# Moving a weight product ahead of the attention in a fused attention and FFN kernel

## The chip, the cores and the metric

The kernel runs on one core of one Trainium2 chip. The time is device microseconds of one execution; the time before is the median of 12 runs. A profile shows one execution: TensorE (PE, with its weight loads as PEld), VectorE (DVE), ScalarE (ACT), GpSimd (POOL), SyncE (SP) and the DMA queues.

## The reference

```python
# q, k, v: 8 batches x 8 heads x 576 positions x 64, fp32
r = max(x, 0);  phi(x) = [r * cos(theta_s), r * sin(theta_s)]      # 128 features per position
kv  = sum over s of phi(k)[s] (x) v[s]        # per batch and head, 128 x 64
den = phi(q) . sum over s of phi(k)[s] + 1e-6
attn = (phi(q) @ kv) / den                    # -> x, 4608 x 512
h = ((x @ w1) * (x @ w2)) @ w3                # w1, w2: 512 x 1024; w3: 1024 x 1024
out = h @ w_out                               # w_out: 1024 x 512; out: 4608 x 512, fp32
```

## The kernel before

The kernel folds the last two products: it computes `w34 = w3 @ w_out` (1024 x 512) once and then, per token, `((x @ w1) * (x @ w2)) @ w34`. All products are in bf16 with fp32 sums.

**Order.** The Tile framework's own scheduling is switched off: each engine runs its instructions in the order in which the program emits them. Tokens are worked in nine blocks of 512 (`t` = 0 to 8). `ffn_groups(t)` is a generator that stops after each group of FFN matmuls; block t has 24 groups, numbered from 0. Groups 0 to 15 of a block make the products with w1 and w2: for feature columns of 128, `aT` with w1 is copied by ACT to `asb`, and DVE multiplies it with `bT` into `abT`. Groups 16 to 23 multiply `abT` with `w34b`, two groups to a row tile, and ACT copies the result to `osb`. The main loop keeps a list of small steps for each group, `slots[g]`, and emits them right behind the group. So the attention of the next batch, and what prepares it, is threaded between the FFN's groups.

**Attention of a batch b.** It goes in five row tiles `c` (four of 128 rows, one of 64): `prep_k` and `prep_q` make the features (the cosine half on DVE, the sine half on ACT, by `features`), `prep_v` copies v beside a column of ones into `va`. `kv_chunk` accumulates k-v sums of eight heads in the PSUM tile `pnum`; its last call copies them to `kvs`. `q_tr` transposes a q tile on PE and copies it to `qpT`; `num` multiplies it with `kvs` and emits the den chain on DVE (add, reciprocal, multiply into `xblk`); `x_tr` transposes `xblk` into the FFN's input `xT`. `pnum` has one buffer, the transposes' tile `pst` two, the FFN's PSUM tile four.

**The start.** Batch 0's k is loaded in fp32 by SP (`kf`); v, q, and the rest are loaded by POOL with a cast to bf16. PE runs 27 idle matmuls on a tile of zeros (`idle_mms`). When k and v are there, batch 0's features and `kv_first()` follow (the k-v sums in two PSUM tiles, copied to `kvs` by ACT in two halves), then the first three q tiles with four more idle matmuls between, and block 0 of the FFN starts. `other_loads` holds back the remaining loads until the first `xblk` is made: the last quarters of w1 and w2, all of w_out in one DMA, w3 in eight row blocks of 128, batches 1 and 2.

**w34.** For each row block `jp` of w3, `w3_tr(jp)` transposes it on PE in eight pieces, DVE copies it to `w3T` (two buffers), and `w34_mm(jp, part)` multiplies it with w_out in two halves of four matmuls; behind the second half ACT copies the sum to `w34b`. Before, all of this stands in block 0 behind group 15 (the first transposes behind group 14), and the features, transposes and k-v sums of batch 1 are threaded between its sixteen halves.

Of the kernel before, what the change touches and what calls it, by code (L numbers as in the profile page):

```python
# [68 lines left out]
def kernel(  # L69
# [26 lines left out]
    ps_att = ctx.enter_context(tc.tile_pool(name="ps_att", bufs=1, space=bass.MemoryType.PSUM))  # L96
    ps_tr = ctx.enter_context(tc.tile_pool(name="ps_tr", bufs=2, space=bass.MemoryType.PSUM))
    first = [ctx.enter_context(ExitStack()) for _ in range(2)]
    ps_idle = first[1].enter_context(tc.tile_pool(name="ps_idle", bufs=1, space=bass.MemoryType.PSUM))
    ps_first = first[0].enter_context(tc.tile_pool(name="ps_first", bufs=1, space=bass.MemoryType.PSUM))  # L100

    ctx.enter_context(tc.manual_schedule())
# [7 lines left out]
    def load_first(eng, t, src, c0=0, n=4, b=0):  # L110
        rows = src[b, :, 0:512, :].rearrange("h (p j) d -> p h j d", j=4)
        eng.dma_start(out=t[:, :, c0:c0 + n, :].rearrange("p h j d -> p h (j d)"),
                      in_=rows[:, :, c0:c0 + n, :].rearrange("p h j d -> p h (j d)"))

    def load_first4(eng, t, src, b=0):
        eng.dma_start(out=t[0:64, :, 4, :], in_=src[b, :, 512:S, :].rearrange("h p d -> p h d"))
# [29 lines left out]
    def load_w3(jp):  # L146
        nc.gpsimd.dma_start(out=w3b[:, jp, :], in_=moe_w3[ts(jp, P), :])

    k0 = raw[0, "k"] = wst.tile([P, H, NCH, D], FP32, name="kf", bufs=1)
    q0 = raw[0, "q"] = ld.tile([P, H, NCH, D], BF16, name="qs")  # L150
    v0 = raw[0, "v"] = ld.tile([P, H, NCH, D], BF16, name="vs")
    load_first(nc.sync, k0, k)
    load_first4(nc.sync, k0, k)
    load_first(nc.gpsimd, v0, v)
    zeros = const.tile([P, 512], BF16, name="zeros")
    nc.vector.memset(zeros[:], 0.0)
    va_bufs, kp_bufs, qp_bufs = [], [], []
# [9 lines left out]
            nc.vector.memset(fp[64:128, 4, :, :], 0.0)  # L167
            bufs.append(fp)

    feature_buffers(0)  # L170
    tiny = const.tile([P, 1], FP32, name="tiny")
    nc.scalar.activation(out=tiny[:], in_=zeros[:, 0:1], func=ACTF.Relu, scale=1.0, bias=0.0)

    unread = ps_idle.tile([P, 512], FP32, name="unread")
    kva = ps_idle.tile([P, 512], FP32, name="kva")

    def idle_mms(n):

        for _ in range(n):
            nc.tensor.matmul(unread[:, :], lhsT=zeros[:, 0:128], rhs=zeros[:], start=True, stop=True)  # L180

    idle_mms(27)
    cosv, sinv = _trig_tables(nc, const)
    identb = const.tile([P, P], BF16, name="identb")
    load_first4(nc.gpsimd, v0, v)
    load_first(nc.gpsimd, q0, q, 0, 2)
    make_identity(nc, identb[:])
    load_first(nc.gpsimd, q0, q, 2, 2)
    def load_w12(c0, n):
        nc.gpsimd.dma_start(out=w1b[:, :, ds(c0, n)], in_=w1v[:, :, ds(c0, n)])  # L190
        nc.gpsimd.dma_start(out=w2b[:, :, ds(c0, n)], in_=w2v[:, :, ds(c0, n)])
# [6 lines left out]
    def other_loads(behind):  # L198

        seen = sm.tile([P, 1], BF16, name="seen", bufs=1)  # L200
        nc.gpsimd.tensor_copy(out=seen[:], in_=behind)
        nc.gpsimd.dma_start(out=w2b[:, :, ds(512, 256)], in_=w2v[:, :, ds(512, 256)])
        load_w12(768, 256)
        nc.gpsimd.dma_start(out=woutb[:], in_=moe_w_out.rearrange("(c p) m -> p c m", p=P))
        for jp in range(8):
            load_w3(jp)
            if jp == 4:
                load(1, "k")
        load(1, "qv")
        load(2, "kqv")  # L210


# [11 lines left out]

    def w34_mm(jp, part):
        if part == 0:
            w34_acc[jp] = ffn_tile()
        acc, w3T = w34_acc[jp], w3Ts[jp]
        for lc in range(4 * part, 4 * part + 4):
            nc.tensor.matmul(acc[:, :], lhsT=w3T[:, lc, :], rhs=woutb[:, lc, :],  # L230
                             start=(lc == 0), stop=(lc == 7))
        if part == 1:
            nc.scalar.copy(out=w34b[:, jp, :], in_=acc[:, :])
# [38 lines left out]
                                        op0=ALU.max, op1=ALU.mult)  # L272

    def prep_k(b, c):
        features(b, feat_of(b)[0], raw[b, "k"], c)

    def prep_q(b, c):
        features(b, feat_of(b)[1], raw[b, "q"], c)
# [10 lines left out]
    def kv_chunk(b, c, i):  # L289
# [8 lines left out]
        if i == NCH - 1:  # L298
# [1 line left out]
            nc.vector.tensor_copy(out=kvs[:].rearrange("p (g h) e -> p g (h e)", g=2),  # L300
                                  in_=kvt[:, :, 0:260])
            att[b]["kvs"] = kvs

    def kv_first():

        kp, qp, va = feat[0]
        kvs = sm.tile([P, H, D + 1], BF16, name="kvs", bufs=2)
        kvb = ps_att.tile([P, 2, 512], FP32, name="pnum")
        halves = (kva[:, :], kvb[:, 0, :])
        for c in range(NCH):  # L310
            for h in range(H):
                nc.tensor.matmul(halves[h // 4][:, ds((h % 4) * 65, 65)], lhsT=kp[:, c, h, :],  # L312
                                 rhs=va[:, c, h, 0:D + 1], start=(c == 0 and h % 4 == 0),
                                 stop=(c == NCH - 1 and h % 4 == 3))
        att_of(0)["kvs"] = kvs
        yield
        for half in range(2):
            nc.scalar.copy(out=kvs[:, 4 * half:4 * half + 4, :], in_=halves[half][:, 0:260])
        yield

    def q_tr(b, c, evac=True):
        R = ROWS[c]
# [117 lines left out]
    def ffn_tile():  # L440
        pool = ps_ffn[ffn_tiles[0] // 2 % 2]
        ffn_tiles[0] += 1
        return pool.tile([P, 512], FP32, name="ffnps")
# [118 lines left out]
            slots[min(last, first + int(i * (last + 1 - first) / len(units)))].append(u)  # L562


    for c in range(NCH):
        prep_k(0, c)
    for c in range(NCH):
        prep_v(0, c)
    kv_steps = kv_first()
    next(kv_steps)  # L570
    q0f = feat[0][1]
    features(0, q0f, q0, 0, scalar_heads=4)
    next(kv_steps)
    prep_q(0, 1)
    idle_mms(2)
    q_tr_halves(0, 0)
    prep_q(0, 2)
    idle_mms(1)
    num(0, 0)
    q_tr(0, 1, evac=False)[1]()  # L580
    other_loads(att[0]["x"][0][:, 0, 0, 0:1])
    features(0, q0f, q0, 3, sin=False)
    q_tr(0, 2, evac=False)[1]()
    features(0, q0f, q0, 3, cos=False)
    idle_mms(1)
    x_tr(0, 0, by_vector=True,
         pst=unread[:, :].bitcast(BF16).rearrange("p (a b) -> p a b", b=128))
    num(0, 1)
    ps_ffn = []
    for stack in first:  # L590
# [5 lines left out]
    for t in range(NT):  # L596
        slots = [[] for _ in range(24)]
        if t == 0:
            slots[1].append(lambda: x_tr(0, 1, by_vector=True))
            slots[1].append(lambda: q_tr(0, 3, evac=False)[1]())  # L600
            slots[1].append(lambda: num(0, 2))
            slots[3].append(lambda: num(0, 3))
            slots[3].append(lambda: x_tr(0, 2))
            slots[5].append(lambda: x_tr(0, 3))
            slots[6].append(lambda: prep_q(0, 4))
            slots[11].append(lambda: feature_buffers(1))
            slots[8].append(lambda: q_tr(0, 4))
            slots[10].append(lambda: num(0, 4))
            slots[12].append(lambda: x_tr(0, 4))
            slots[14].append(lambda: w3_tr(0))  # L610
            between = [[] for _ in range(32)]
            later = [[] for _ in range(24)]
            spread(prep_units(1, (prep_k,)), 6, 8, between)
            spread(prep_units(1, (prep_q,)), 10, 12, between)
            spread(prep_units(1, (prep_v,)), 13, 13, between)
            attention_at(1, between, kv=(14, 14, 14, 14, 15), tr=(12, 13, 17, 18, 19),
                         nu=(16, 17, 18, 20, 22), xt=(18, 19, 20, 22, 25))
            later[:8] = between[24:32]
            for jp in range(8):
                for part in range(2):  # L620
                    if part == 0 and jp < 7:
                        slots[15].append(lambda jp=jp: w3_tr(jp + 1))
                    slots[15].append(lambda jp=jp, part=part: w34_mm(jp, part))
                    slots[15] += between[2 * jp + part]
            for g in range(16, 24):
                slots[g] += between[g]
            slots[16].append(open_held)
            slots[16].append(lambda: load(3, "kqv"))
            spread(prep_units(2, (prep_k,)), 20, 23, slots)
        elif t == 1:  # L630
            for g in range(24):
                slots[g] += later[g]
            spread(prep_units(2, (prep_q,)), 0, 4, slots)
            spread(prep_units(2, (prep_v,)), 0, 4, slots)
            attention_at(2, slots, kv=(2, 3, 4, 5, 6), tr=(3, 5, 7, 9, 11),
                         nu=(8, 10, 12, 14, 16), xt=(8, 10, 12, 14, 16))
            slots[4].append(lambda: load_piece(4, 0, feat[2][1], 3))
            spread(interleaved(3, range(1, 6)), 6, 23, slots)
        else:
            if t + 1 < B:  # L640
                attention_at(t + 1, slots, kv=(0, 1, 2, 3, 4), tr=(2, 4, 7, 10, 13),
                             nu=(6, 8, 10, 12, 14), xt=(6, 8, 10, 12, 14))
            for g in {5: (3, 9, 15, 20), 6: (1, 6, 11, 16)}.get(t, ()):
                slots[g].append(store_held)
            if t + 2 < B:
                spread(interleaved(t + 2), 0, 22, slots)
        for g, _ in enumerate(ffn_groups(t)):
            for u in slots[g]:
                u()
# [30 lines left out]
```

## Time and profile before

| | us |
|---|---|
| median of 12 runs (lowest to highest) | 251.63 (251.08 to 253.7) |
| profiled execution, its own time | 251.62 |
| its span, first to last instruction | 249.3 |
| busy in the span: PE, DVE, ACT, POOL | 241.3, 141.4, 124.3, 90.0 |
| first FFN matmul | 15.70 |
| first matmul of token block 1 | 63.42 |
| mean granted clock of TensorE over the span | 0.997 |

The span leaves out 2.3 us of the execution's time. Busy times of PE are modelled ends of pipelined matmuls. All times in the text are counted from the start of the span.

### The profile page before, as it was taken

The numbers are of one execution on the slowest core, as the hardware profiler recorded it, in microseconds if no ns is written. First come the engines' busy times: TensorE is split into PE (matmuls) and PEld (weight loads), VectorE is DVE, ScalarE is ACT, GpSimd is POOL, SyncE is SP. The second block draws the span as 40 slices with busy tenths as digits, with TensorE's granted clock in tenths as the row PEclk, the third lists the DMA queues.
The fourth block names the chain that finished last, engine by engine and source line by source line (L and its number), as shares of the span: only waits on it lengthen the run. The fifth ranks groups of instructions, "written<-read, shape, count | busy, mean of one in ns | idle before, by whom it ended". The sixth has DMA issues, their size and how long they took to land.

```text
span 249.3 us, 4941 instructions
## 1 busy us (share of the span) xinstructions
PE 241.3 (97%) x1847; PEld 130.1 (52%) x1879; DVE 141.4 (57%) x338; ACT 124.3 (50%) x209; POOL 90.0 (36%) x171
## 2 busy tenths in 40 slices
PE   8899999999999999999999999999999999999994
PEld 3578555666555455445544554555455544444443
DVE  7875665657889529905981695189227704312321
ACT  2676316915966656465655555555432242323320
POOL 7665154540533613441443327271342540023000
PEclk9999999999999999999999999999999999999998
DMA  7999999999999999999899979999699982014013
GB/s 194 182 194 201 208 204 205 198 199 198 269 137 169 181 170 130 173 199 171 127 129 190 182 100 188 146 186 192 130 141 196 266 232 64 3 32 136 1 44 127
DMA packets 80760, 39.85 MB, mean 160 GB/s; under 512 B 48224, under 2 KB 77280, under 8 KB 80736
## 3 DMA queue, kind: packets, MB, share of 16 engines
q0 software_dynamic: 37024, 27.20, 71.2%
q1 hardware_dynamic: 43280, 11.87, 31.7%
q10 hardware_dynamic: 432, 0.46, 0.5%
q8 instruction: 15, 0.25, 0.4%
q14 instruction: 9, 0.07, 0.1%
HBM read 38.80 MB, written 9.44 MB: 193 GB/s over the span
## 4 chain that ended last, share of the span: by engine, by line
PE 93%; DMA 2%; ACT 2%; issue 1%; DVE 1%; ACTq 0%
PE ffnps L462 49%; PE ffnps L508 24%; PE ffnps L230 5%; PE pnum L353 4%; PE pnum L295 4%; DMA kf<-in_k_dram 2%; PE pst L326 2%; PE pst L218 1%; ACT kp L267 1%; PE pst L390 1%; PE ffnps L531 1%; PE kva L312 0%; DVE xblk L363 0%; PE pnum L312 0%; PE pfirst L353 0%
## 5 line engine op out<-in xcount | busy, mean ns | idle before, releaser
L503 DVE TENSOR_TENSOR abT<-asb,ffnps 128x512 bf16<-128x512 bf16 x68 | 46.4, 683 | 71.4 <-PE ffnps L462 70.6
L462 PE MATMUL ffnps<-xT,w1b 128*128 128x512 bf16 (+2 forms) x313 | 74.4, 357 | 0.7 <-ACT xT L392 0.2
L462 PE MATMUL ffnps<-xT,w2b 128*128 128x512 bf16 (+2 forms) x305 | 73.1, 356 | 0.7
L499 ACT CAST asb<-ffnps 128x512 bf16<-128x512 f32 x68 | 39.8, 585 | 61.7 <-PE ffnps L462 56.1
L508 PE MATMUL ffnps<-w34b,abT 128*128 128x512 bf16 x274 | 62.4, 379 | 0.3
L462 PEld LDWEIGHTS <-w1b 128*128 128x128 bf16 x320 | 29.4, 98 | 29.6 <-issue 0.6
L508 PEld LDWEIGHTS <-abT 128*128 128x128 bf16 x280 | 26.8, 98 | 31.2
L462 PEld LDWEIGHTS <-w2b 128*128 128x128 bf16 x320 | 26.9, 98 | 20.3
L267 ACT ACTIVATE qp<-qs,sinv 128x512 bf16<-128x512 bf16 (+2 forms) x40 | 28.3, 718 | 1.6 <-DMA qs<-in_q_dram 1.6
L363 DVE TENSOR_TENSOR xblk<-pnum,den 128x512 bf16<-128x512 f32 (+1 forms) x39 | 26.9, 691 | 1.4
L287 POOL COPY va<-vs 128x512 bf16<-128x512 bf16 (+1 forms) x30 | 18.3, 622 | 20.3 <-DMA vs<-in_v_dram 11.6
L436 POOL DMA_DIRECT2D out_dram<-osb x20 | 10.6, 533 | 41.3 <-ACT osb L518 41.3
L267 ACT ACTIVATE kp<-ks,sinv 128x512 bf16<-128x512 bf16 (+1 forms) x35 | 24.7, 721 | 0.0
L518 ACT COPY osb<-ffnps 128x512 f32<-128x512 f32 x19 | 11.1, 584 | 21.9 <-PE ffnps L508 19.9
L353 PEld LDWEIGHTS <-qpT 128*128 128x128 bf16 x320 | 15.1, 98 | 8.6 <-issue 0.9
L295 PEld LDWEIGHTS <-kp 128*128 128x128 bf16 x280 | 13.1, 98 | 7.1
L263 DVE TENSOR_SCALAR qp<-qs,cosv 128x512 bf16<-128x512 bf16 (+1 forms) x40 | 16.2, 411 | 0.6 <-DMA qs<-in_q_dram 0.6
L518 ACT COPY held<-ffnps 128x512 f32<-128x512 f32 x16 | 9.4, 585 | 14.4 <-PE ffnps L508 14.4
L353 PE MATMUL pnum<-kvs,qpT 128*128 128x65 bf16 x312 | 16.5, 194 | 0.0
L544 POOL COPY seen<-kp 128x1 bf16<-128x1 bf16 (+1 forms) x20 | 3.7, 186 | 33.3 <-DVE kp L263 25.6
L230 PE MATMUL ffnps<-woutb,w3T 128*128 128x512 bf16 x61 | 15.0, 379 | 0.1
L436 POOL DMA_DIRECT2D out_dram<-held x22 | 11.6, 535 | 8.2 <-DMA out_dram<-osb 6.5
(88 smaller groups left out, 197.3 us busy)
## 6 DMA issues: line engine op xcount, KB each, us to landing
out_dram<-held POOLq DMA_DIRECT2D x10, 256.0 KB, 5.3
qs<-in_q_dram POOLq DMA_DIRECT2D x8, 256.0 KB, 7.9
w3b<-in_moe_w_dram POOLq DMA_DIRECT2D x8, 256.0 KB, 13.5
ks<-in_k_dram POOLq DMA_DIRECT2D x6, 320.0 KB, 10.7
qs<-in_q_dram POOLq DMA_DIRECT2D x6, 320.0 KB, 9.0
vs<-in_v_dram POOLq DMA_DIRECT2D x6, 320.0 KB, 8.7
ks<-in_k_dram POOLq DMA_DIRECT2D x6, 256.0 KB, 9.0
vs<-in_v_dram POOLq DMA_DIRECT2D x6, 256.0 KB, 9.5
```

Source lines behind the costliest of these rows:

```text
L230: nc.tensor.matmul(acc[:, :], lhsT=w3T[:, lc, :], rhs=woutb[:, lc, :], start=(lc == 0), stop=(lc == 7))
L267: nc.scalar.activation(out=dst[:R, c, 0:n, D:F], in_=src[:R, 0:n, c, :], func=ACTF.Relu, scale=sinv[:R, at:at + 1], bias=0.0)
L287: eng.tensor_copy(out=feat_of(b)[2][:R, c, :, 0:D], in_=raw[b, "v"][:R, :, c, :])
L295: nc.tensor.matmul(kvt[:, h // 4, ds((h % 4) * 65, 65)], lhsT=kp[:, c, h, :], rhs=va[:, c, h, 0:D + 1], start=(i == 0 and h % 4 == 0), sto ...
L353: nc.tensor.matmul(nt[:, h // 4, ds((h % 4) * 65, 65)], lhsT=qpT[:, h, ds(at, 128)], rhs=kvs[:, h, :], start=True, stop=True)
L363: nc.vector.tensor_tensor(out=xblk[rows], in0=n4[:, :, :, 0:D], in1=den[rows].unsqueeze(3).to_broadcast([R, 2, 4, D]), op=ALU.mult)
L436: eng.dma_start(out=rows[:, :, cols], in_=osb[64 * i:64 * i + rows.shape[0], :, cols])
L462: nc.tensor.matmul(out, lhsT=w[:, kc, ts(jc, 128)], rhs=x[:, kc, tok], start=(kc == 0), stop=(kc == 3))
L499: nc.scalar.copy(out=asb[:], in_=aT[:, :])
L503: nc.vector.tensor_mul(out=abT[:, jc, :], in0=asb[:], in1=bT[:, :])
L508: nc.tensor.matmul(ops[:, :], lhsT=abT[:, jc, ts(ms, 128)], rhs=w34b[:, jc, :], start=(jc == 0), stop=(jc == 7))
L518: nc.scalar.copy(out=osb[:, ms % 2, :], in_=ops[:, :])
```

## The change

`w34` is computed first. PE runs 12 idle matmuls, then the transposes and products of w3's row blocks as they arrive; batch 0's features, k-v sums and q tiles follow behind block 6, with the second half of block 7's product between the first q transposes and the first `num`. `kv_first()` is gone, and batch 0 uses `kv_chunk` like the others, with one copy to `kvs` on DVE. Its k comes by POOL with a cast, like v and q; of the k sines ACT makes six heads and DVE two. The first four row blocks of w_out (half of it) are loaded in fp32 by SP and cast by four ACT copies, the other four by POOL with a cast. POOL's order is w3 blocks 0 and 1, half of w_out, w3 blocks 2 to 6, k, w3 block 7, v, q, then w1 and w2 as before. The two sets of feature buffers (`feature_buffers`, memsets on DVE) are made between the blocks. In block 0 the features of batch 1 stand in groups 9 to 16, its k-v sums in 13 to 15, and its q transposes in 16 to 19. The w34 sums have a PSUM pool of their own (`ps_w34`, two buffers) that is given back, with the tile of the first `num`, before the FFN's tiles are made.

```diff
+    woutf = wst.tile([P, 4, DM], FP32, name="woutf", bufs=1)
+    woutv = moe_w_out.rearrange("(c p) m -> p c m", p=P)
+    for half in range(2):
+        nc.sync.dma_start(out=woutf[:, ts(half, 2), :], in_=woutv[:, ts(half, 2), :])
+    load_w3(0)
+    k0, q0, v0 = (ld.tile([P, H, NCH, D], BF16, name=name + "s") for name in "kqv")
-    load_first(nc.sync, k0, k)
-    load_first4(nc.sync, k0, k)
-    load_first(nc.gpsimd, v0, v)
...
-    idle_mms(27)
+    idle_mms(12)
+    load_w3(1)
+    identb = const.tile([P, P], BF16, name="identb")
+    make_identity(nc, identb[:])
+    nc.gpsimd.dma_start(out=woutb[:, 4:8, :], in_=woutv[:, 4:8, :])
     cosv, sinv = _trig_tables(nc, const)
+    for lc in range(4):
+        nc.scalar.copy(out=woutb[:, lc, :], in_=woutf[:, lc, :])
+    for jp in range(2, 7):
+        load_w3(jp)
+    load_first(nc.gpsimd, k0, k)
+    load_first4(nc.gpsimd, k0, k)
+    load_w3(7)
+    load_first(nc.gpsimd, v0, v)
     load_first4(nc.gpsimd, v0, v)
     load_first(nc.gpsimd, q0, q, 0, 2)
     load_first(nc.gpsimd, q0, q, 2, 2)
...
-        nc.gpsimd.dma_start(out=woutb[:], in_=moe_w_out.rearrange("(c p) m -> p c m", p=P))
-        for jp in range(8):
-            load_w3(jp)
-            if jp == 4:
-                load(1, "k")
-        load(1, "qv")
+        load(1, "kvq")
         load(2, "kqv")
...
-        features(b, feat_of(b)[0], raw[b, "k"], c)
+        features(b, feat_of(b)[0], raw[b, "k"], c, scalar_heads=6 if b == 0 else H)
...
-    for c in range(NCH):
-        prep_k(0, c)
+    w3_tr(0)
+    w3_tr(1)
+    w34_mm(0, 0)
+    w34_mm(1, 0)
+    w34_mm(0, 1)
+    w3_tr(2)
+    w34_mm(1, 1)
+    feature_buffers(0)
+    for jp in range(2, 7):
+        w3_tr(jp + 1)
+        w34_mm(jp, 0)
+        w34_mm(jp, 1)
+        if jp == 3:
+            feature_buffers(1)
+        if jp == 5:
+            for c in range(NCH):
+                prep_k(0, c)
+    w34_mm(7, 0)
     for c in range(NCH):
         prep_v(0, c)
-    kv_steps = kv_first()
-    next(kv_steps)
-    q0f = feat[0][1]
+        kv_chunk(0, c, c)
+    q0f = feat_of(0)[1]
     features(0, q0f, q0, 0, scalar_heads=4)
-    next(kv_steps)
     prep_q(0, 1)
-    idle_mms(2)
     q_tr_halves(0, 0)
     prep_q(0, 2)
-    idle_mms(1)
+    w34_mm(7, 1)
     num(0, 0)
...
-            spread(prep_units(1, (prep_k,)), 6, 8, between)
-            spread(prep_units(1, (prep_q,)), 10, 12, between)
-            spread(prep_units(1, (prep_v,)), 13, 13, between)
...
+            spread(prep_units(1, (prep_k,)), 9, 11, slots)
+            spread(prep_units(1, (prep_v,)), 12, 13, slots)
+            spread(prep_units(1, (prep_q,)), 14, 16, slots)
+            attention_at(1, later, kv=(13, 13, 14, 14, 15), tr=(16, 17, 17, 18, 19),
+                         nu=(17, 18, 19, 20, 22), xt=(19, 20, 21, 22, 25))
```

In the lines left out, `w34_mm` takes its PSUM tile from `ps_w34`, the last idle matmul goes, and the first `x_tr` takes its tile from `ps_w34` too.

More of the change, by code (lines that the diff above doesn't have):

```diff
@@ L98 @@
     first = [ctx.enter_context(ExitStack()) for _ in range(2)]
-    ps_idle = first[1].enter_context(tc.tile_pool(name="ps_idle", bufs=1, space=bass.MemoryType.PSUM))
+    ps_w34 = first[1].enter_context(tc.tile_pool(name="ps_w34", bufs=2, space=bass.MemoryType.PSUM))
     ps_first = first[0].enter_context(tc.tile_pool(name="ps_first", bufs=1, space=bass.MemoryType.PSUM))
@@ L147, in load_w3 @@
         nc.gpsimd.dma_start(out=w3b[:, jp, :], in_=moe_w3[ts(jp, P), :])
-    k0 = raw[0, "k"] = wst.tile([P, H, NCH, D], FP32, name="kf", bufs=1)
-    q0 = raw[0, "q"] = ld.tile([P, H, NCH, D], BF16, name="qs")
-    v0 = raw[0, "v"] = ld.tile([P, H, NCH, D], BF16, name="vs")
-    load_first(nc.sync, k0, k)
-    load_first4(nc.sync, k0, k)
-    load_first(nc.gpsimd, v0, v)
+    woutf = wst.tile([P, 4, DM], FP32, name="woutf", bufs=1)
[4 more added lines that the diff above has]
+    k0, q0, v0 = (ld.tile([P, H, NCH, D], BF16, name=name + "s") for name in "kqv")
+    raw.update({(0, "k"): k0, (0, "q"): q0, (0, "v"): v0})
     zeros = const.tile([P, 512], BF16, name="zeros")
@@ L168, in feature_buffers @@
             bufs.append(fp)
-    feature_buffers(0)
     tiny = const.tile([P, 1], FP32, name="tiny")
     nc.scalar.activation(out=tiny[:], in_=zeros[:, 0:1], func=ACTF.Relu, scale=1.0, bias=0.0)
-    unread = ps_idle.tile([P, 512], FP32, name="unread")
-    kva = ps_idle.tile([P, 512], FP32, name="kva")
+    unread = ps_w34.tile([P, 512], FP32, name="acc")
     def idle_mms(n):
@@ L180, in idle_mms @@
             nc.tensor.matmul(unread[:, :], lhsT=zeros[:, 0:128], rhs=zeros[:], start=True, stop=True)
-    idle_mms(27)
-    cosv, sinv = _trig_tables(nc, const)
-    identb = const.tile([P, P], BF16, name="identb")
+    idle_mms(12)
[3 more added lines that the diff above has]
+    nc.gpsimd.dma_start(out=woutb[:, 4:8, :], in_=woutv[:, 4:8, :])
+    cosv, sinv = _trig_tables(nc, const)
+    for lc in range(4):
[6 more added lines that the diff above has]
+    load_first(nc.gpsimd, v0, v)
     load_first4(nc.gpsimd, v0, v)
     load_first(nc.gpsimd, q0, q, 0, 2)
-    make_identity(nc, identb[:])
     load_first(nc.gpsimd, q0, q, 2, 2)
@@ L226, in w34_mm @@
         if part == 0:
-            w34_acc[jp] = ffn_tile()
+            w34_acc[jp] = ps_w34.tile([P, 512], FP32, name="acc")
         acc, w3T = w34_acc[jp], w3Ts[jp]
@@ L302, in kv_chunk @@
             att[b]["kvs"] = kvs
[L304 to L309, printed above, removed]
-        for c in range(NCH):
[L311 to L319, printed above, removed]
     def q_tr(b, c, evac=True):
@@ L562, in spread @@
             slots[min(last, first + int(i * (last + 1 - first) / len(units)))].append(u)
-    for c in range(NCH):
-        prep_k(0, c)
+    w3_tr(0)
[16 more added lines that the diff above has]
+    w34_mm(7, 0)
     for c in range(NCH):
         prep_v(0, c)
-    kv_steps = kv_first()
-    next(kv_steps)
-    q0f = feat[0][1]
+        kv_chunk(0, c, c)
+    q0f = feat_of(0)[1]
     features(0, q0f, q0, 0, scalar_heads=4)
-    next(kv_steps)
     prep_q(0, 1)
-    idle_mms(2)
     q_tr_halves(0, 0)
     prep_q(0, 2)
-    idle_mms(1)
+    w34_mm(7, 1)
     num(0, 0)
@@ L584 @@
     features(0, q0f, q0, 3, cos=False)
-    idle_mms(1)
     x_tr(0, 0, by_vector=True,
-         pst=unread[:, :].bitcast(BF16).rearrange("p (a b) -> p a b", b=128))
+         pst=ps_w34.tile([P, 512], FP32, name="acc")[:, :].bitcast(BF16).rearrange("p (a b) -> p a b", b=128))
     num(0, 1)
@@ L605 @@
             slots[6].append(lambda: prep_q(0, 4))
-            slots[11].append(lambda: feature_buffers(1))
             slots[8].append(lambda: q_tr(0, 4))
@@ L609 @@
             slots[12].append(lambda: x_tr(0, 4))
-            slots[14].append(lambda: w3_tr(0))
-            between = [[] for _ in range(32)]
-            later = [[] for _ in range(24)]
-            spread(prep_units(1, (prep_k,)), 6, 8, between)
-            spread(prep_units(1, (prep_q,)), 10, 12, between)
-            spread(prep_units(1, (prep_v,)), 13, 13, between)
[L616 to L626, printed above, removed]
+            later = [[] for _ in range(32)]
+            spread(prep_units(1, (prep_k,)), 9, 11, slots)
[3 more added lines that the diff above has]
+                         nu=(17, 18, 19, 20, 22), xt=(19, 20, 21, 22, 25))
+            for g in range(24):
+                slots[g] += later[g]
+            later = later[24:]
             slots[16].append(open_held)
@@ L630 @@
         elif t == 1:
-            for g in range(24):
-                slots[g] += later[g]
+            for g, units in enumerate(later):
+                slots[g] += units
             spread(prep_units(2, (prep_q,)), 0, 4, slots)
```

## The prediction

> **What bounds it now.** I read the page first, then stretches, then the chain of waits, then single engines.
>
> ```profile
> PE 241.3 (97%) x1847; PEld 130.1 (52%) x1879; DVE 141.4 (57%) x338; ACT 124.3 (50%) x209; POOL 90.0 (36%) x171
> PE 93%; DMA 2%; ACT 2%; issue 1%; DVE 1%; ACTq 0%
> 0.00:15.70 15.70, 13.17 (x114) 6.91 (x116) 12.20 (x42) 8.59 (x14) 9.93 (x22) 1.00 1.27 190
> 15.70:63.40 47.70, 47.04 (x474) 30.99 (x481) 31.09 (x75) 24.52 (x43) 19.80 (x31) 1.00 1.34 201
> 32.00:50.00 18.00, 17.84 (x141) 10.63 (x143) 11.25 (x27) 10.71 (x18) 8.97 (x14) 1.00 1.29 202
> ```
>
> TensorE (PE) is busy 97% and is 93% of the chain, so only PE work removed, or PE waiting, moves the end. In the stretches the columns after the length are PE, its weight loads, DVE, ACT, POOL. From 15.7 us on PE is full. Before 15.7 most of its 13.17 us is the idle matmuls (L180), which do nothing. The row 32 to 50 is where w3 @ w_out is computed, with batch 1's preparation between: DVE has 7 us free there and ACT 7 us.
>
> ```profile
> 0.74 6.14 DMA kf<-in_k_dram
> 6.97 3.18 ACT kp L267 x5
> ...
> 15.70 1.05 PE ffnps L462 x16
> ...
> 33.52 0.45 PE pst L218 x8
> 33.97 1.73 PE ffnps L230 x8
> ...
> 63.42 1.73 PE ffnps L462 x8
> ```
>
> This chain (start, length, what) gives the frame. The FFN starts at 15.70, token block 1 at 63.42. One block of w3 costs PE 0.45 + 1.73 = 2.18 us, all eight 17.4 us. The change takes these out of block 0 and puts them ahead of the FFN. If nothing else moved, the FFN could start at 15.70 + 17.4 = **33.1 us** with the end unchanged. That is the break-even.
>
> **When w3 arrives.** POOL issues a further cast DMA when an older one has landed, so its waits show the pace of the queue:
>
> ```profile
> 24.56 0.69 POOL L134 DMA_DIRECT2D ks<-in_k_dram  x1 [0.64 <-DMA w2b<-in_moe_w_dram]
> 30.31 0.56 POOL L147 DMA_DIRECT2D w3b<-in_moe_w_dram  x1 [5.07 <-DMA woutb<-in_moe_w_out_dram]
> 31.53 0.55 POOL L147 DMA_DIRECT2D w3b<-in_moe_w_dram  x1 [0.65 <-DMA w3b<-in_moe_w_dram]
> 32.78 0.53 POOL L147 DMA_DIRECT2D w3b<-in_moe_w_dram  x1 [0.71 <-DMA w3b<-in_moe_w_dram]
> ```
>
> All of w_out took 30.31 - 24.56 = 5.75 us, a w3 block 1.25 us. The DMA issues give the start: v's 512 KB is issued at 1.28 and lands 8.3 us later, at 9.6, beside 1,152 KB of fp32 k from SP. After the change the same time holds 1,024 KB of fp32 w_out from SP and w3 blocks 0 and 1 (512 KB): 0.4 us for the 128 KB less, 0.2 us for w3's better pace, so about 9.0. Then half of w_out by cast, 5.75 / 2 = 2.9, and block 2: 9.0 + 2.9 + 1.25 = **13.1 us**. Until then PE has two blocks' transposes and three half products, 0.9 + 2.6 = 3.5 us. SP's fp32 half costs transfer time like the cast half (1,024 KB at the 390 GB/s that the DMA row shows while k comes: 2.7 us), and ACT's four casts (0.58 us each by the w34b copies) lie in its idle time before 11 us.
>
> **The chain after block 2.** Blocks come every 1.25 us and cost PE 2.18, so from 13.1 PE runs through. Six transposes 2.7 us and twelve half products (all but the three done and the last, which stands behind the first q transposes) 12 x 0.86 = 10.4 us: 26.2 us. One wait comes in. The rows that price DVE:
>
> ```profile
> L220 DVE COPY w3T<-pst 128x1024 bf16<-128x1024 bf16 x8 | 5.5, 690 | 5.9 <-PE pst L218 5.8
> L263 DVE TENSOR_SCALAR kp<-ks,cosv 128x512 bf16<-128x512 bf16 x8 | 2.4, 340 | 0.0
> L300 DVE CAST kvs<-pnum 128x520 bf16<-128x520 f32 x1 | 0.7, 700 | 2.0 <-PE pnum L295 2.0
> ```
>
> In DVE's order prep_k(0) stands between the copies w3T(6) and w3T(7): five cosines of 0.34 and five sines of two heads, estimated at 0.2 (four heads took 0.28), 2.7 us. Block 6's transposes end at 13.1 + 8.3 = 21.4, its copy at 22.3, prep_k at 25.0, w3T(7) at 25.7. PE wants it at 25.3: 0.4 us lost. Behind it on PE stand block 7's first half, which ends at 26.6, and the k-v products. kv_chunk(0) adds 1.3 (32 of 40 such matmuls took 1.02): 27.9. ACT's five k sines of six heads (0.6 each) start behind w34b(5) at 23.9 and end at 27.0, just in time. kvs is now one DVE copy, 0.2 + 0.70, ahead of the q features: 28.8. Before, q's first cosine started at 11.45 and the FFN at 15.70, 4.25 us later; the half product of 0.86 where one idle matmul of 0.2 stood adds 0.25 net of waits. FFN start **33.3 us**.
>
> The DMAs are no limit here: blocks 3 to 6 by 18.1, k (576 KB, 3.3) 21.4, block 7 22.7, v 26.0, the first half of q at 27.3, needed at 28.8. w1 and w2 follow q in the same order as before. The memsets of feature_buffers (1.4 us a set) lie beside 1.73 us of products. POOL issues a block in 0.55 us and moves it in 1.25, so issuing is no limit, and k's move from SP to POOL is paid in the 3.3 above. Removing 19 of 31 idle matmuls gains nothing by itself; PE waits instead.
>
> **The clock.** Idle matmuls stood 0.43 us apart up to 5.4 us and 0.21 after, so the array doubles its pace once kept busy. At the end it falls back:
>
> ```profile
> 244.40:247.70 3.30, 1.31 (x20) 1.10 (x18) 1.01 (x3) 0.17 (x1) 0.00 (x0) 1.00 0.50 165
> 247.80:249.20 1.40, 0.00 (x0) 0.00 (x0) 0.00 (x0) 0.00 (x0) 0.00 (x0) 0.50 0.00 0
> ```
>
> The granted clock (third number from the end) is 0.50 after a stretch 40% busy that ended 2 us after the last matmul. The 12 idle matmuls end near 6 us; from there to 9.4 us PE has 0.9 us of transposes, 26%. I expect one fall to half somewhere between 7 and 13 us. It costs nothing where products then wait for block 2 anyway, up to 1.1 us where it reaches past 13.1; I take 0.3: FFN at **33.6**, 0.5 us behind break-even.
> The Trainium skill (TensorE: Matmul & The Clock Gate, Part 1) says that the array is throttled after an idle window of about 3.4 us. The gap here is shorter, so by that rule alone this term would be zero and the forecast 253.1.
>
> **Block 0 without its cover.** Batch 1's features, 10 on ACT (0.72 each) and 10 on DVE with five v copies (0.28), ran beside w34's light load; now they stand in groups 9 to 16 beside the FFN's own copies. In times of before: DVE starts the first full-width abT at 27.42 and does, ahead of the v copies that kv_chunk(1) reads first, two abT (1.38), four k cosines (1.4), the den chain of batch 0's last tile (0.17 + 0.20 + 0.69), then v and v (0.56): with hand-overs it is at 32.3. PE is there at 31.25 and would be done at 31.8, now 32.6: **0.8 us**, between 0 (ACT or DVE a little earlier) and 1.2. ACT's k sines stand ahead of the asb copy of group 12 (0.7 late) and its q sines ahead of the first osb; the PSUM tiles behind them are wanted four groups later, so this costs nothing. In groups 16 to 23 two q transposes more (0.9, only moved) meet DVE's five qpT copies, kvs and four den chains, 8 us of DVE in 12, with one pnum buffer; before this stretch lost 0.3 us, I add **0.5** (0 to 1.2). Batch 1's k, v and q land 0.7 to 2 us ahead of need if w2's last pieces follow the xblk signal as before: k 42.9, v 45.9, q 49.0. Batch 2's loads end within 0.3 us of before (52), since the total bytes of the queue hardly change. Blocks 1 to 8 are the same instructions.
>
> **Sum.** Break-even miss 0.5 + 0.8 + 0.5 = 1.8 us. The profiled execution took 251.62 us (span 249.3 and 2.3 around it), which is the median's 251.63: 251.6 + 1.8 = **253.4 us**. About 0.3% (0.75 us) is what a measurement of this kernel can tell from no change. Unknowns: DMA start 0.6 either way, clock -0.3 to +0.8, block 0 -1.1 to +1.1.
>
> **Rivals.**
> *The DMA queue sets the FFN's start and PE gains.* If the DVE and kvs waits are swallowed, q's landing at 27.3 + 4.5 gives FFN 31.8, and with block 0's stalls absent the sum is -1.3: 250.3 us. For it: the 9.3 us of idle PE before 10.2. Against: PE's own queue of 2.18 us per block. 0.13.
> *A wash.* FFN at 33.1 to 33.6 with batch 1 fitting: about 251.9. For it: ACT and DVE are only half busy from 15.7 to 32. 0.14.
> *The clock stays low.* If the array is at half until 18 us, PE does in the 4.9 us behind block 2 what takes 2.45 at full pace: +2.45 in place of 0.3, 255.6. It decides from the moment that half pace lasts beyond 14 us, since nothing behind block 2 waits for data. 0.10.
> *The forecast*, 0.63, mostly slower; 0.06 of it ends within the bound.
>
> Faster 0.13, same 0.20, slower 0.67. The range 251.0 to 255.6 takes in the wash and most of the clock case.
>
> **To check after.** w3T(7)'s copy ending at 25.7; first FFN matmul (now L450) at 33.6; clock 0.50 for a stretch between 7 and 13; PE waiting about 0.8 us for va before batch 1's L300; token block 1 at about 65.2. An FFN start below 32.5, or no PE wait at L300, makes this wrong on the fast side; a half clock past 15 us on the slow side.

## The result and the profile after

| | before | after |
|---|---|---|
| median, us (runs) | 251.43 (49, beside all runs of this study) | 252.61 (12; 252.16 to 252.84) |
| profiled execution, us | 251.62 | 252.66 |
| its span, us | 249.3 | 250.4 |
| first FFN matmul, us | 15.70 | 32.50 |
| first matmul of token block 1 (PE rows), us | 63.26 | 63.98 |
| block 0 of the FFN, us | 47.56 | 31.48 |

The time is 1.0041 of the time before, 95% interval 1.0028 to 1.0054. The forecast was 253.4 us, which is 1.007 of the execution that it was made against. So the change makes the kernel slower, by 1.0 us by this ratio and by 1.2 by the two medians, where 1.8 were expected. The starts of block 1 are those of PE's rows; the chain of waits puts them 0.16 us later, at 63.42 and 64.14.

The page of the kernel after, busy times and the chain's shares, and then its windows (columns: length, PE, weight loads, DVE, ACT, POOL, granted clock, DMA share, GB/s), cut where the FFN and block 1 start:

```profile
PE 238.4 (95%) x1829; PEld 127.8 (51%) x1860; DVE 140.6 (56%) x344; ACT 125.3 (50%) x211; POOL 91.3 (36%) x173
PE 79%; DMA 9%; DVE 6%; issue 2%; POOL 2%; ACT 1%; DVEq 0%; POOLq 0%
0.00:32.50 32.50, 26.91 (x221) 14.69 (x225) 18.85 (x60) 14.36 (x24) 16.22 (x33) 1.00 1.24 196
32.50:63.98 31.48, 30.09 (x348) 21.00 (x352) 23.60 (x63) 19.64 (x35) 14.93 (x22) 1.00 1.42 198
63.98:250.40 186.42, 181.40 (x1261) 92.12 (x1283) 98.12 (x223) 91.31 (x154) 60.19 (x119) 1.00 0.98 146
```

PE is 79% of the chain now, where it was 93%; DMA has gone from 2% to 9% and DVE from 1% to 6%. Block 0 (the second window) is less full: PE idles 1.4 of 31.5 us there. Before, when batch 1's preparation ran beside the product that makes w34, it idled 0.7 of 47.6.

The chain of waits of the kernel after (start, length, what):

```profile
5.34 10.17 DMA w3b<-in_moe_w_dram
15.79 11.58 DMA qs<-in_q_dram
27.39 1.13 ACT qp L272 x2
28.63 0.61 PE pst L327 x8
32.50 1.05 PE ffnps L450 x16
48.56 0.67 PE pnum L300 x16
54.38 0.70 DVE qpT L316
55.13 0.43 PE pnum L341 x8
64.14 1.73 PE ffnps L450 x8
```

This chain reaches the FFN's start through the DMA queue: a w3 block lands, POOL then issues q, q lands at 27.37, ACT makes two sines, and the FFN begins 5.1 us after the landing. But the second of these sines belongs to the next q tile, and the first transposes need DVE's first cosine too, which starts at 28.14 (rows below). What that cosine waits for is PE's own queue, as the forecast had it; e4_kvs_act below takes the two paths apart. Behind the start, in block 0, stand DVE pieces that were not on the chain before.

POOL's rows show how the queue moved; in brackets is what ended the idle time before an issue:

```profile
7.29 0.90 POOL L112 DMA_DIRECT2D ks<-in_k_dram  x1 [0.34 <-DMA w3b<-in_moe_w_dram]
12.03 0.56 POOL L147 DMA_DIRECT2D w3b<-in_moe_w_dram  x1 [2.73 <-DMA woutb<-in_moe_w_out_dram]
13.23 0.89 POOL L112 DMA_DIRECT2D vs<-in_v_dram  x1 [0.65 <-DMA w3b<-in_moe_w_dram]
15.79 0.88 POOL L112 DMA_DIRECT2D qs<-in_q_dram  x1 [0.62 <-DMA w3b<-in_moe_w_dram]
```

w3 block 2 landed at 12.94 (13.1 forecast), block 7 at 22.83 (22.7), the last of v at 25.94 (26.0), q's first half at 27.37 (27.3). q's issue waits for a w3 block to land, as w3's did before. The queue could be forecast to 0.2 us from the costs of single DMAs in the profile before.

The next rows are DVE around the step where the forecast saw a wait, and PE beside it:

```profile
24.45 0.67 DVE L225 COPY w3T<-pst 128x1024 bf16<-128x1024 bf16 x1
27.53 0.70 DVE L305 CAST kvs<-pnum 128x520 bf16<-128x520 f32 x1 [0.79 <-PE pnum L300]
28.14 0.34 DVE L268 TENSOR_SCALAR qp<-qs,cosv 128x512 bf16<-128x512 bf16 x1
23.45 2.77 PE L235 MATMUL acc<-woutb,w3T 128*128 128x512 bf16 x12
28.63 0.61 PE L327 MATMUL pst<-identb,qp 128*128 128x128 bf16 x8 [1.15 <-ACT qp L272]
```

The copy w3T(7) ends at 25.12, not at 25.7, and PE's twelve matmuls (three half products) run from 23.45 without a gap. PE's rows show no idle time from block 2's transposes at 12.99 to the end of the k-v sums at 27.49, and the kvs copy starts at 27.53, as soon as these sums are done. q is there at 27.37, but DVE does its first cosine at 28.14, behind the kvs copy, and PE has nothing for 1.15 us. The page puts this wait down to ACT's sine; the cosine ends at 28.48, 0.15 us before the transposes.

### The profile page after: what moved, and what is told of

Its sections match the earlier page's. It is cut to its first block, busy times and chain, and to the rows that moved or that the text cites. A ratio compares the mean times of both kernels' runs of the same rounds, so it can differ in the third digit from the quotient of the medians.

```text
span 250.4 us, 4917 instructions
## 1 busy us (share of the span) xinstructions
PE 238.4 (95%) x1829; PEld 127.8 (51%) x1860; DVE 140.6 (56%) x344; ACT 125.3 (50%) x211; POOL 91.3 (36%) x173
## 4 chain that ended last, share of the span: by engine, by line
PE 79%; DMA 9%; DVE 6%; issue 2%; POOL 2%; ACT 1%; DVEq 0%; POOLq 0%
PE ffnps L450 45%; PE ffnps L496 23%; DMA qs<-in_q_dram 5%; DMA w3b<-in_moe_w_dram 4%; PE pnum L300 4%; PE pnum L341 4%; DVE xblk L351 2%; DVE abT L491 1%; PE pst L314 1%; DVE kp L268 1%; POOL w3b L147 1%; DVE qpT L316 1%; PE ffnps L519 1%; DVE den L350 1%; PE pst L378 1%
## 5 line engine op out<-in xcount | busy, mean ns | idle before, releaser
L272 ACT ACTIVATE kp<-ks,sinv 128x512 bf16<-128x512 bf16 (+3 forms) x40 | 27.4, 707 | 0.0
L506 ACT COPY osb<-ffnps 128x512 f32<-128x512 f32 x19 | 11.1, 584 | 22.9 <-PE ffnps L496 22.8
L300 PEld LDWEIGHTS <-kp 128*128 128x128 bf16 x320 | 14.5, 98 | 8.2 <-ACT xT L380 0.9
L268 DVE TENSOR_SCALAR qp<-qs,cosv 128x512 bf16<-128x512 bf16 (+1 forms) x40 | 16.8, 426 | 0.0
L300 PE MATMUL pnum<-va,kp 128*128 128x65 bf16 x320 | 15.7, 193 | 0.5 <-DVE va L292 0.4
L235 PE MATMUL acc<-woutb,w3T 128*128 128x512 bf16 x61 | 14.9, 379 | 1.1 <-DMA woutb<-in_moe_w_out_dram 1.0
L268 DVE TENSOR_SCALAR kp<-ks,cosv 128x512 bf16<-128x512 bf16 (+1 forms) x40 | 14.3, 368 | 0.1
```

The source lines that it names most:

```text
L268: nc.vector.tensor_scalar(out=dst[:R, c, :, 0:D], in0=src[:R, :, c, :], scalar1=0.0, scalar2=cosv[:R, at:at + 1], op0=ALU.max, op1=ALU.mult)
L272: nc.scalar.activation(out=dst[:R, c, 0:n, D:F], in_=src[:R, 0:n, c, :], func=ACTF.Relu, scale=sinv[:R, at:at + 1], bias=0.0)
L300: nc.tensor.matmul(kvt[:, h // 4, ds((h % 4) * 65, 65)], lhsT=kp[:, c, h, :], rhs=va[:, c, h, 0:D + 1], start=(i == 0 and h % 4 == 0), sto ...
L506: nc.scalar.copy(out=osb[:, ms % 2, :], in_=ops[:, :])
```

## Experiments

All are edits of the kernel after. "Block 0" is the time from the first FFN matmul to the first one of block 1.

**Batch 1's k-v sums a group later (e2_kv14).** The forecast put 0.8 us of block 0's cost on PE waiting for `va`.

```diff
-            attention_at(1, later, kv=(13, 13, 14, 14, 15), tr=(16, 17, 17, 18, 19),
+            attention_at(1, later, kv=(14, 14, 14, 14, 15), tr=(16, 17, 17, 18, 19),
```

> Batch 1's first k-v sums stand one FFN group later (kv in groups 14, 14, 14, 14, 15 in place of 13, 13, 14, 14, 15). Theory: in the changed kernel PE lost 0.57 us before the first of them because DVE had the v copies behind two abT and a den chain. With the group between, that wait falls below 0.15, token block 1 starts at 63.5 in place of 64.0, and the time is about 0.5 us less than that of the changed kernel, ratio to before 1.002. Rival: DVE is the bound of the whole stretch, the wait comes back at the next hand-over (the first num of batch 1), and the ratio stays at 1.004.

Measured: 251.97 us, 1.0027 of before (1.0014 to 1.0039). Block 0 took 31.15 us instead of 31.48. The wait of 0.57 us before the first sums is gone, but one of 0.25 us stands before the fourth tile's, where DVE makes an abT between the v copies; the one before `num` stayed at 0.5. So the wait came back in part, as the rival had it, and the ratio lies between the two.

**The second q transpose a group earlier as well (e3_kv14_tr16).**

```diff
-            attention_at(1, later, kv=(13, 13, 14, 14, 15), tr=(16, 17, 17, 18, 19),
+            attention_at(1, later, kv=(14, 14, 14, 14, 15), tr=(16, 16, 17, 18, 19),
```

> As e2, and batch 1's second q transpose stands in group 16 in place of 17, so that a group of matmuls lies between it and the first num that needs its copy. Theory: the wait of 0.5 us before that num falls to about 0.15, block 1 starts at 63.2, ratio to before 1.001. Rival: DVE's queue (kvs, q cosines, two qpT copies) is late anyway and the wait is only moved; block 1 starts where e2 has it.

Measured: 251.84 us, 1.0023 (1.0006 to 1.0039); block 0 took 30.78 us. PE's rows, in the kernel after and then in this one:

```profile
48.56 0.67 PE L300 MATMUL pnum<-va,kp 128*128 128x65 bf16 x16 [0.41 <-DVE va L292]
55.13 0.43 PE L341 MATMUL pnum<-kvs,qpT 128*128 128x65 bf16 x8 [0.34 <-DVE qpT L316]
```

```profile
48.99 1.33 PE L300 MATMUL pnum<-va,kp 128*128 128x65 bf16 x32
54.37 0.43 PE L341 MATMUL pnum<-kvs,qpT 128*128 128x65 bf16 x8
56.30 0.43 PE L341 MATMUL pnum<-kvs,qpT 128*128 128x65 bf16 x8 [0.20 <-DVE xblk L351]
59.87 0.43 PE L341 MATMUL pnum<-kvs,qpT 128*128 128x65 bf16 x8 [0.15 <-DVE xblk L351]
```

The first sums and the first `num` have no wait any more; 0.15 us is left before the fourth tile's sums. Two waits for `xblk` stay, which is what the single `pnum` buffer costs here. So 0.7 of block 0's 1.3 us is a matter of where three small steps are put, and not of the missing cover as such. The timed intervals of this kernel and of the kernel after overlap; the traces carry the reading.

**kvs off DVE (e4_kvs_act).** Batch 0's `kvs` is copied by ACT in two halves behind its first q sine.

```diff
-            nc.vector.tensor_copy(out=kvs[:].rearrange("p (g h) e -> p g (h e)", g=2),
-                                  in_=kvt[:, :, 0:260])
+            if b > 0:
+                nc.vector.tensor_copy(out=kvs[:].rearrange("p (g h) e -> p g (h e)", g=2),
+                                      in_=kvt[:, :, 0:260])
...
     features(0, q0f, q0, 0, scalar_heads=4)
+    for half in range(2):
+        nc.scalar.copy(out=att[0]["kvs"][:, 4 * half:4 * half + 4, :],
+                       in_=att[0]["kv"][:, half, 0:260])
```

> The kvs copy of batch 0 goes back to ACT in two halves behind the first q sine, so DVE starts q's first cosine when q lands. Theory: in the changed kernel q landed at 27.4 and DVE's cosine began at 28.1, behind the kvs copy; now the FFN starts at 31.8 in place of 32.5 and the time is 0.7 us less, ratio to before 1.0015. Rival: the FFN's start is held by w2's first quarter (landed at 31.5) or by the half product of block 7 that stands before the first num; then it starts at 32.2 or later and the ratio is 1.003 or more.

Measured: 251.47 us, 1.0008 (0.9997 to 1.0018). The chain of waits of this kernel:

```profile
15.86 11.36 DMA qs<-in_q_dram
27.24 0.35 DVE qp L268
27.80 0.62 PE pst L328 x8
31.68 1.05 PE ffnps L451 x16
```

q lands and DVE's cosine starts on it at once, 0.9 us earlier than in the kernel after. The FFN starts 0.82 us earlier, 4.44 us behind the cosine (4.36 in the kernel after). The start now follows q's landing. That it did not before is seen when runs are put side by side (us; ACT's first q sine starts at once on q's landing):

| run | kvs copy on | first k-v sum | first q sine | FFN's start | behind the sum | behind the sine |
|---|---|---|---|---|---|---|
| after | DVE | 26.06 | 27.39 | 32.50 | 6.44 | 5.11 |
| e2_kv14 | DVE | 26.26 | 27.42 | 32.70 | 6.44 | 5.28 |
| e6_wout_cast | DVE | 27.88 | 28.85 | 34.33 | 6.45 | 5.48 |
| e8_cast_idle26 | DVE | 27.06 | 28.29 | 33.50 | 6.44 | 5.21 |
| e4_kvs_act | ACT | 26.13 | 27.24 | 31.68 | 5.55 | 4.44 |
| e5_best | ACT | 26.15 | 27.66 | 32.10 | 5.95 | 4.44 |
| e7_best_again | ACT | 26.22 | 27.50 | 31.94 | 5.72 | 4.44 |

With kvs on DVE the FFN starts 6.44 or 6.45 us behind PE's first k-v sum, whenever q lands (so it does in e1_idle2, e3_kv14_tr16, p3_after and p4_after); with kvs on ACT it starts 4.44 us behind q's sine, wherever the sums stand. So in the kernel after PE's queue set the start, by way of the kvs copy, and q's landing takes over only when that copy leaves DVE.

**Both (e5_best, and the same kernel again as e7_best_again).**

> e3 and e4 together. Theory: the two gains lie in different stretches and add: FFN at 31.8, block 1 at 62.5, against 63.26 before, ratio to before 0.997 to 0.999. Rival: the stretch from 44 to 62 is held by DMA landings of batch 1's k, v and q, which do not move with the FFN's start; then part of what e4 gains is lost again and the ratio is 1.000 to 1.002.

> The kernel of e5 once more (kv and q transposes one place apart, kvs on ACT), beside the other runs of this call, to see whether it beats the kernel before: theory 0.9975 (FFN 31.7 to 32.1, block 1 at 62.5 to 62.9 against 63.26), upper end of the interval below 1. Rival: its first figure was a lucky chip, and the ratio is 0.999 to 1.001.

Measured: 250.76 us, 0.9974 (0.9957 to 0.9991), and 250.85 us, 0.9978 (0.9963 to 0.9994). This kernel is faster than the kernel before and than the kernel after. In e5_best the FFN starts at 32.10, 0.3 us later than expected, since q landed later. Windows of the second run, cut at its FFN start and its block 1:

```profile
0.00:31.94 31.94, 26.25 (x225) 14.49 (x225) 18.11 (x59) 14.67 (x26) 16.22 (x33) 1.00 1.23 196
31.94:62.66 30.72, 30.13 (x353) 21.13 (x353) 23.68 (x63) 19.66 (x35) 15.11 (x22) 1.00 1.43 198
62.66:248.90 186.24, 182.65 (x1285) 92.20 (x1283) 97.89 (x223) 91.33 (x154) 60.16 (x119) 1.00 1.03 147
```

Block 0 takes 30.72 us, PE idle for 0.6 of them, no more than before; break-even was 47.56 - 17.4 = 30.2. The start is 1.2 us ahead of the break-even of 33.1.

**Idle matmuls taken away (e1_idle2).** The theory was that the twelve idle matmuls keep the clock at full for the first products.

```diff
-    idle_mms(12)
+    idle_mms(2)
```

> The changed kernel with 2 idle matmuls in place of 12. Theory on the clock: the array is then at half pace when w3's block 0 is transposed at 7 us and stays there until it has been busy for a while; the first half products at 8.8 us take 1.7 us each in place of 0.86, and PE is 1 to 3 us late behind block 2, where nothing waits for data any more. FFN start 33.5 to 35.5 in place of 32.5, ratio to before 1.008 to 1.016. Rival: the first products wait for w_out's second half (11.7 us) anyway and PE has slack against q's landing at 27.4, as in the run with kvs on ACT, where the clock was at half for a stretch between 6 and 14 us and the FFN still began 4.4 us after q landed; then the FFN starts within 0.3 us of 32.5 and the ratio stays near 1.004.

Measured: 252.54 us, 1.0035 (1.0021 to 1.0049), like the kernel after; the theory fell. PE's rows of this kernel, then of the kernel after:

```profile
6.99 1.03 PE L223 MATMUL pst<-identb,w3b 128*128 128x128 bf16 x8 [4.76 <-DMA w3b<-in_moe_w_dram]
9.17 3.97 PE L235 MATMUL acc<-woutb,w3T 128*128 128x512 bf16 x12
13.00 0.62 PE L223 MATMUL pst<-identb,w3b 128*128 128x128 bf16 x8
```

```profile
7.05 0.62 PE L223 MATMUL pst<-identb,w3b 128*128 128x128 bf16 x8 [0.76 <-DMA w3b<-in_moe_w_dram]
8.82 1.99 PE L235 MATMUL acc<-woutb,w3T 128*128 128x512 bf16 x8
11.79 1.02 PE L235 MATMUL acc<-woutb,w3T 128*128 128x512 bf16 x4 [0.98 <-DMA woutb<-in_moe_w_out_dram]
12.99 0.62 PE L223 MATMUL pst<-identb,w3b 128*128 128x128 bf16 x8 [0.18 <-DMA w3b<-in_moe_w_dram]
```

At half pace eight transposes take 1.03 us instead of 0.62 and twelve matmuls of the product 3.97 (2.6 at full pace). But at full pace PE waits 0.98 us for w_out's second half and again for block 2, so both reach block 2's transposes at 13.0, and the FFN starts at 32.49 and 32.50.

**All of w_out by POOL's cast queue (e6_wout_cast).**

```diff
-    woutf = wst.tile([P, 4, DM], FP32, name="woutf", bufs=1)
...
-    for half in range(2):
-        nc.sync.dma_start(out=woutf[:, ts(half, 2), :], in_=woutv[:, ts(half, 2), :])
     load_w3(0)
+    nc.gpsimd.dma_start(out=woutb[:, 0:4, :], in_=woutv[:, 0:4, :])
...
-    for lc in range(4):
-        nc.scalar.copy(out=woutb[:, lc, :], in_=woutf[:, lc, :])
```

> The changed kernel with all of w_out by cast DMAs from POOL (first half behind w3's block 0, second behind block 1), no fp32 half from SP and no ACT casts. Theory of the prediction: the fp32 half costs the DMA engines 2.7 us and its cast twin 2.9, so block 2 and q land 0.2 us later, plus what SP moved before POOL's first packets, some 0.4 us: FFN at 32.8 to 33.1, ratio 1.005 to 1.007. Rival: SP's queue brings bytes that POOL's alone would not have (two queues side by side are faster than one); then q lands 1.5 us or more later and the ratio is 1.009 or more. Other side: the cast queue alone is as fast from the start, ratio 1.004 or less.

Measured: 254.34 us, 1.0118 (1.0093 to 1.0142). The FFN starts at 34.33, 1.83 us later; q lands 1.45 us later, w3 block 2 0.92. That is close to what the rival expected (1.5 us, 1.009 or more) and far from the theory. First a row of this kernel's windows (to 6 us, and where the first products stand), then that of the kernel after:

```profile
0.00:6.00 6.00, 4.79 (x20) 1.91 (x20) 1.03 (x5) 1.49 (x2) 4.79 (x16) 1.00 0.49 73
11.00:14.60 3.60, 3.60 (x10) 1.26 (x9) 0.46 (x1) 0.00 (x0) 1.06 (x3) 0.53 1.16 211
```

```profile
0.00:6.00 6.00, 4.80 (x12) 1.64 (x12) 1.67 (x9) 3.11 (x5) 4.79 (x17) 1.00 0.70 214
```

In the first 6 us the cast queue alone moves 73 GB/s; with SP's fp32 half beside it, 214. Later it moves some 200 GB/s alone. What each queue moved up to 4.7 us (packets, MB, share), in the kernel after and then in this one, is:

```profile
q1 hardware_dynamic: 505, 1.00, 59.0%
```

```profile
q0 software_dynamic: 154, 0.27, 36.2%
```

q1 carries SP's load, q0 POOL's casts, and these are all the queues that moved anything by then. POOL issued its first cast DMA at 1.27 us in both kernels. Alone, the cast queue moved nothing up to 2.7 us and 136 GB/s from there to 4.7. Beside SP's load, which ran at 407 GB/s in that window, it moved nothing at all up to 4.7. So SP's half does not run in a gap of the cast queue; it goes first, earlier and faster. Its 1.00 MB of fp32 are 0.50 MB in bf16, 0.23 more than the cast queue had brought (its bytes are counted in bf16: a block of 256 KB in each 1.25 us is some 210 GB/s, as the windows have it). At that pace 0.23 MB are 1.1 us, an estimate; w3 block 2 lands 0.92 earlier. The Trainium skill (DMA: Bandwidth & Descriptors, "Issuing engines are not separate DMA queues") says that starting DMAs from several engines saves only the time to issue them. Block 2 is indeed issued 0.76 us earlier with SP's half, but it lands 8.7 us behind its issue, and blocks land 1.25 us apart where POOL issues one in 0.55, so the issue is not what it waits for. No run moves the issue alone.

The clock in this kernel is at half from 11 to 14.6 us (0.53), and PE is busy all of that time, so the half pace may have had a cost of its own.

**The same with 26 idle matmuls (e8_cast_idle26).**

```diff
-    idle_mms(12)
+    idle_mms(26)
```

> All of w_out by the cast queue as in e6, with 26 idle matmuls in place of 12, so that TensorE is busy up to some 8.5 us and its clock stays at full speed past 11. In e6 TensorE ran without a wait from 10.11 us (w3 block 1's transposes) to the k-v sums, and twelve half products took 4.44 us at half clock where 2.6 would do, so that block 2, landed at 13.86, was transposed only from 14.84. If the half clock had a cost of its own there, block 2 is now transposed from 13.9, the FFN starts at 33.3 to 33.4 (1.0 us earlier, at q's landing of 28.8 plus 4.4 to 4.5) and the time is about 253.3. The rival, that e6's lateness is only that of the data and the clock costs nothing, expects the FFN at 34.3 and 254.3 again.

Measured: 254.20 us (four runs), 1.0108 (1.0048 to 1.0168), by its time alone not told apart from e6_wout_cast: the median stands where the rival had it (254.3), the profiled execution, at 253.40 the fastest of the four, where the theory had it. PE's rows of e6_wout_cast, then of this kernel:

```profile
10.57 4.44 PE L231 MATMUL acc<-woutb,w3T 128*128 128x512 bf16 x12
14.84 0.61 PE L219 MATMUL pst<-identb,w3b 128*128 128x128 bf16 x8
```

```profile
10.52 1.99 PE L231 MATMUL acc<-woutb,w3T 128*128 128x512 bf16 x8
12.66 1.02 PE L231 MATMUL acc<-woutb,w3T 128*128 128x512 bf16 x4 [0.16 <-DMA woutb<-in_moe_w_out_dram]
13.89 0.62 PE L219 MATMUL pst<-identb,w3b 128*128 128x128 bf16 x8 [0.21 <-DMA w3b<-in_moe_w_dram]
```

At full clock block 2 is transposed as it lands, 0.95 us earlier, and the FFN starts at 33.50 instead of 34.33. In the profiled executions the 1.83 us of e6_wout_cast are thus about 1.0 us of later data and 0.8 us of half clock. One execution of each carries this split.

**Two further profiles of each kernel (p1_before, p2_before, p3_after, p4_after).** The profile after lost a further 0.35 us in block 4 (23.63 us against 23.28). The question is whether that belongs to the change.

> The kernel before once more. Block 1's first product to the end stays near 186 us if a late transposed x (a wait of 0.3 to 1.0 us of TensorE for xT) is rare here; the rival, that such a wait falls on both kernels alike, expects it in one of two looks here as often as in the changed kernel. Span 249 to 250 us.

> The kernel before, a second further look, the same expectations as for the first: token block 1 in 24.4 us and blocks 2 to 5 in 23.3 us each if the late transposed x is rare in it; one block longer by 0.3 to 1.0 us if it falls on both kernels alike.

> The changed kernel once more. If the late transposed x belongs to the change, one of blocks 1 to 4 is longer than in the kernel before by 0.3 to 1.0 us, as block 4 was by 0.35 us in its first profile; if it is chance, blocks 1 to 5 take 24.4 and four times 23.3 us in at least one of the two looks.

> The changed kernel, a second further look, the same expectations as for the first: a wait of TensorE for xT behind a DMA transpose in block 1 or 4 if it belongs to the change, worth 0.3 to 1.0 us; none, and blocks of 24.4 and 23.3 us, if it is chance that falls on both kernels.

Measured: 250.88, 251.38, 252.15 and 252.04 us. Blocks 1 to 5 of both further profiles of the kernel after took 24.4 and four times 23.3 us; one block of p2_before was 0.10 us longer. So block 4's 0.35 us is not a fixed part of the change. Block 1 starts at 63.26, 63.05 and 63.46 in the three profiles of before and at 63.98, 64.24 and 64.10 after: 0.85 us apart on the mean. So 0.85 of the medians' 1.18 us lies ahead of block 1, where the change is. The rest is not accounted for; single executions have waits there. e1_idle2, for one, spent 0.82 us at the end of its block 1 waiting for a transposed x:

```profile
89.39 0.82 PE L450 MATMUL ffnps<-xT,w1b 128*128 128x512 bf16 x3 [0.82 <-DMA xT<-xblk]
```

Block 1 of e6_wout_cast and e8_cast_idle26 is 0.8 us longer as well; none of the three profiles of the kernel before has such a block 1, and none of the three of the kernel after. Why the DMA transpose comes late in some executions, and whether it does so more often after the change, stays open.

## Why the prediction was nearly right

The direction was right and the time lies in the forecast's range, but the sum of 0.5 + 0.8 + 0.5 came from two terms of which one had the wrong sign. That the time came so near is in part luck: block 1 starts 0.72 us later in the profiled execution, 0.85 on the mean of three, and not 1.8; the rest of the 1.0 to 1.2 us measured lies behind block 1, where the sum had nothing.

**The FFN's start: forecast 0.5 us behind break-even, measured 0.6 ahead** (32.50 against 33.1). This stands at the bound of 32.5 below which the forecast called itself wrong. The path was right: PE's queue from block 2 on, the k-v sums, the kvs copy, q's cosine. The error is 33.6 - 32.5 = 1.1 us, and it lies in the sizes of the steps. The DVE wait before w3T(7), 0.4 us, did not come; the copy ended 0.06 us before PE reached the product that needs it (25.18), so this was close. Five pairs of cosine and sine were priced at 2.7 us by adding the durations of single operations, but in DVE's rows the next one starts before the one before has ended, and the ten took 22.09 to 24.45, 2.36 us. The hand-over to `kvs` was taken at 0.2 us and was 0.04 (the sums end at 27.49), the first cosine started 0.09 before the copy ended, and the products ended 0.14 early, as block 2 landed early; the k-v sums took 1.43 us where 1.3 stood. Together, 0.4 + 0.16 + 0.09 + 0.14 - 0.13, that is the 0.66 us by which DVE reached q early (28.14 against 28.8). The clock's 0.3 us was not lost in this execution, in which the clock did not fall; e1_idle2 shows that half pace up to 11.6 us costs nothing here. Three of the twelve timed runs have a mean granted clock of 0.993, the mean that e4_kvs_act has with one stretch at half (8.46 to 11.88 us); their times, 252.58 to 252.68, lie among the others. The last 0.14 us is the 4.36 us from cosine to FFN, where 4.5 stood.

**Block 0: forecast 1.3 us, measured 1.3** (31.48 against 30.2). The wait for `va` was 0.57 us (0.8 forecast) and the stretch of `num` had 0.50, 0.2 and 0.3 (0.5 forecast above the old 0.3). e2 and e3 showed that both waits are where the forecast put them. In the two further profiles this term was 1.4.

**SP's half of w_out.** Its transfer was priced well (1,024 KB in 2.7 us at 390 GB/s; 407 were measured), but "like the cast half" is wrong: with a cast half in its place block 2 lands 0.92 us later, since the cast queue starts later and slower. It did no harm to the sum, since block 2's time had been taken from the old k load by SP in the same place.

**The rivals.** "The DMA queue sets the FFN's start" did not hold in the kernel after, because its condition, that the kvs wait is swallowed, did not: the cosine stood 0.77 us behind q's landing. Its price was right: 27.3 + 4.5 = 31.8 was its number, and e4 measured 31.68 as soon as kvs left DVE. With the block's stalls repaired too, e5 and e7 came to 250.8, near its 250.3. "The clock stays low" was not seen in the kernel after, but half pace has a price where nothing waits for data: 0.8 us at the FFN's start in the profiled execution of e6 against that of e8, which their medians do not confirm. "A wash" had the FFN's start at 33.1 to 33.6 and no cost in block 0; neither held.

The Trainium skill (TensorE: Matmul & The Clock Gate, Part 1) puts the clock's decisions on a free-running window of about 3.4 us. The clock's records in the traces agree: it rose to full at 5.96 us and fell at 251.72, behind the last instruction, in the profile after, 72 times 3.413 us apart, and 5.43 and 247.78 before, 71 times. The rise came at 5.96, 6.70 and 5.81 us in the three profiles of the kernel after, so the window falls differently in each. That may be why some executions show a fall and others do not; no run tests it.

## What to carry to other kernels

Moving work ahead of the first dependent stage gains only the idle time that it fills; what it had covered must be looked for in the stage that it leaves, and here that stage's waits cost more than the start had gained, until three steps were moved by a group and one copy went to an idle engine. When a stage begins with a transfer's landing, ask what the engine that first touches that data has queued just ahead of it: one 0.70 us copy on DVE, which itself waited for PE's sums, held the start back by 0.82 us. A wait that the profile puts down to one engine can belong to another; several runs side by side show which event the start keeps its distance from. Sum short DVE operations by the distance between their starts, not by their durations.

## What the hardware showed that was not expected

- The cast queue on POOL moved nothing up to 2.7 us and 136 GB/s from there to 4.7, some 200 later. A plain load by SP ran at 407 GB/s from 2.7 to 4.7, and beside it the cast queue moved nothing up to 4.7 us, though its first DMA was issued at 1.27. SP's half of w_out is worth about 1.0 us at the FFN's start (32.50 against 33.50 in e8_cast_idle26).
- Half clock costs by what the products wait for and not by how long it lasts: nothing in e1_idle2 (up to 11.6 us, with data missing until 12.9), and 0.8 us in the profiled execution of e6_wout_cast (11.1 to 14.6 us, with block 2 there from 13.86).
- Where the clock is at half from the start, the granted clock in the page and the windows reads 1.00: e1_idle2's mean is 0.999, with matmuls at half pace. The durations of matmuls show it.
